# Large matrix products that read their moving operand in turn from the two halves of each row (attention and feed-forward, one core)

## The chip, the cores and the metric

The kernel runs on one core of a Trainium2 chip. The metric is device time in microseconds (us) of one execution. The unchanged kernel takes 863.88 us, the median of three runs (862.88 to 864.18).

## The reference

```python
def _attn_ref(q, k, v):                      # batch 8, heads 8, 576 rows, 64 columns
    q_s = softmax of q over its 64 columns
    k_s = softmax of k over the 576 rows
    kv = np.einsum('bhsd,bhse->bhde', k_s, v)
    return np.einsum('bhsd,bhde->bhse', q_s, kv)

def _moe_ref(x, w_in, w_out):                # x 4608 x 512, w_in 512 x 2048, w_out 2048 x 512
    h = np.maximum(x @ w_in, 0.0)
    return (h * h @ w_out)
```

The heads of the attention's output are put side by side, which gives x with 8 x 576 = 4608 rows of 512. All numbers are float32.

## The kernel before, in words

Nearly all of the time goes to the two products of the feed-forward part. Each float32 operand is split into a high and a low part of the type float32r, and a product is made of three matmuls, high times high, high times low and low times high. Every such matmul has a stationary operand of 128 x 128 (`lhsT`, loaded by its own LDWEIGHTS) and a moving operand of 128 x 512 (`rhs`), and adds into one PSUM bank of 128 x 512.

The batch is worked off in two ways.

- Tiles t = 0 to 6 are the first 512 rows of batches 0 to 6. For each tile a loop runs over the 16 blocks f of 128 hidden columns. `first_part` makes h (128 hidden columns x 512 rows of x) with x as the moving operand, `first` applies the relu and squares, `split_g` splits the square into `gh` and `gl`, and `second` adds into four banks `acc[c]` (128 rows of x each) with a block of 128 columns of `gh` or `gl` as the stationary operand and `w_out` (tile `w`, 512 output columns) as the moving one. `store` copies `acc[c]` to SBUF (tile `o`, on VectorE or ScalarE) and sends it to memory. The attention of the next tiles is worked in between.
- The remaining 1024 rows (batch 7 and the last 64 rows of the others) go through a seven-product scheme on quarters of the matrices. In the pair stage `product` (six matmuls, source line 1264) makes quarter products in the banks `z.A` and `z.B`; `pair_p1` to `pair_p7` copy them out on ScalarE (tile `u`) or add them on VectorE (tile `c`). In the closing stage `product_step` (twelve matmuls for two calls, source line 1780) does the same for `w_out` in the banks `out`; `copies`, `added` and `turned` take the results out, `turned` by a VectorE transpose that is followed by the stores.

The order of the work of tile 0 is made by a planner in the file (`Planner`, with fixed costs and a list of seeds); the rest stands in the order of the code. Engines wait for each other by semaphores alone. Matmuls that go through the planner's helper show source line 100, so tile names tell them apart: `h<-xh,w`, `h<-xl,w` (first product), `acc<-w,gh`, `acc<-w,gl` (second), `h<-...` at L1264 (pairs) and `out<-...` at L1780 (closing stage).

Of the kernel before, what the change touches and what calls it, by code (L numbers as in the profile page):

```python
# [15 lines left out]
AF = mybir.ActivationFunctionType  # L16
ALU = mybir.AluOpType
# [319 lines left out]
def attention_ffn(  # L337
# [26 lines left out]
    B, H, SQ, D = q.shape  # L364
    DM = H * D
    DF = w_in.shape[1]
    P = 128
    C = 4
    M = C * P
    TL = SQ - M  # L370
# [34 lines left out]
    TB = 2  # L405
# [3 lines left out]
    WT = B - 1  # L409
# [22 lines left out]
    V, S, G = Engine(plan, nc.vector, 0.14, 0.00108), Engine(plan, nc.scalar, 0.18, 0.00087), Engine(plan, nc.gpsimd, 0.1, 0.0021)  # L432
    T, Y = Engine(plan, nc.tensor, 0.013, 1 / 2400), Engine(plan, nc.sync, 0.1, 0.0)

    const.pool.tile([P, 32], F32, tag="pad", name="pad")
    ident = const.pool.tile([P, P], F32, tag="ident", name="ident")
    make_identity(nc, ident)
    ones = const.pool.tile([P, P], F32, tag="ones", name="ones")  # L440
# [33 lines left out]
    halves = [("i", f) for f in range(LA)]  # L474
# [63 lines left out]
    made = {}  # L538
# [490 lines left out]
    def first_part(t, f, x, p):  # L1029
        if p == 0:  # L1030
            made["h", f] = (
                View(Buffer(None, [P, M], F32, None, f"h_{t}_{f}", choices=[(ps_o, f"o{C - 1}")]))
                if t == 0 and f == LA else ps_h.tile([P, M], F32, tag="h", name=f"h_{t}_{f}")
            )
        xh, xl = x[p]
        with plan.together(True):
            for i, (w, m) in enumerate(((wi_h, xh), (wi_h, xl), (wi_l, xh))):
                T.matmul(
                    out=made["h", f], lhsT=w[f][:, p * P:(p + 1) * P], rhs=m,
                    start=(p == 0 and i == 0), stop=(p == NP - 1 and i == 2),  # L1040
                )
        if t == 0 and p == 0:
            plan.mark(f)
# [26 lines left out]
    def second(f, parts, acc, c, begin=0, end=NF - 1):  # L1070
        gh, gl = parts
        cs = slice(c * P, (c + 1) * P)
        with plan.together(True):
            for n, (a, w) in enumerate(((gh, wo_h), (gh, wo_l), (gl, wo_h))):
                T.matmul(
                    out=acc[c], lhsT=a[:, cs], rhs=w[f],
                    start=(f == begin and n == 0), stop=(f == end and n == 2),
                )

# [180 lines left out]
    def product(out, w, x, begin, end=True):  # L1260
        (wh, wl), (xh, xl) = (w[:, 0, :], w[:, 1, :]), x
        for k in range(2):
            for i, (a, m) in enumerate(((wh, xh), (wh, xl), (wl, xh))):
                nc.tensor.matmul(  # L1264
                    out=out.real(), lhsT=a[:, k * P:(k + 1) * P].real(), rhs=m[k].real(),
                    start=(begin and k == 0 and i == 0), stop=(k == 1 and i == 2),
                    skip_group_check=True,
                )

    def store(t, acc, c):  # L1270
        if c % 2 == 0:
            made["o"] = cvt.tile([P, 2, DM], F32, tag="w", name=f"o_{t}_{c}")
        o = made["o"][:, c % 2, :]
        if t == B and c == C - 1:
            V.tensor_copy(out=o[:, 0:DM // 2], in_=acc[c][:, 0:DM // 2])
            S.copy(out=o[:, DM // 2:DM], in_=acc[c][:, DM // 2:DM])
        elif c % 2 or 0 < t < WT - 1 and c == 0:
            S.copy(out=o, in_=acc[c])
        else:
            V.tensor_copy(out=o, in_=acc[c])  # L1280
        if t < B:
            rows = out[t * SQ:t * SQ + M, :].rearrange(
                "(p c) e -> p c e" if t < TB else "(c p) e -> p c e", c=C
            )
            Y.dma_start(out=rows[:, c, :], in_=o)
        else:
            per = P // TL
            for j in range(per):
                r0 = (c * per + j) * SQ + M
                queue = S if c == C - 1 and j % 2 else Y  # L1290
                queue.dma_start(out=out[r0:r0 + TL, :], in_=o[j * TL:(j + 1) * TL, :])


    load_kq(0, 0, "k")
# [295 lines left out]
    for t in range(WT):  # L1590
        x_next, acc = begin_next(t), begin_acc(t)
        parts = {}
        for f in range(NF):
            todo = turns[t, f]
            h = first(t, f, x)
# [75 lines left out]
    def pair_p1(z):  # L1671
        product(z.A, z.w["a11"], x_of["b11"], True)
        z.u1 = temp("xh2", f"u1_{z.n}")
        S.copy(out=z.u1, in_=z.A)

    def pair_p2(z):
        product(z.B, z.w["a12"], x_of["b21"], True)
        c = ffn.tile([P, M], F32, tag="r", name=f"c11_{z.n}")
        V.tensor_tensor(out=c, in0=z.B, in1=z.u1, op=ALU.add)
        square(c, V)  # L1680
        keep("b12", z.n, c)

    def pair_p6(z):
        product(z.A, z.w["s2"], x_of["t2"], False)
        z.u2 = temp(("xl2", "xl3")[z.n % 2], f"u2_{z.n}")
        S.copy(out=z.u2, in_=z.A)

    def pair_p5(z):
        product(z.B, z.w["s1"], x_of["t1"], True)
# [1 line left out]
    def pair_p7(z):  # L1691
        product(z.A, z.w["s3"], x_of["t3"], False)
        u3 = temp("xh3", f"u3_{z.n}")
        S.copy(out=u3, in_=z.A)
        c = temp("ek", f"c22_{z.n}", att, 2)
        V.tensor_tensor(out=c, in0=z.B, in1=u3, op=ALU.add)
        own_sums(z.n + 1, w_of.get(z.n + 1), 5)
        S.activation(out=c, in_=c, func=AF.Relu)
        square(c, S)
        keep("b21", z.n, c)  # L1700

    def pair_p4(z):
        product(z.A, z.w["a22"], x_of["t4"], False)
        c = ffn.tile([P, M], F32, tag="gh", name=f"c21_{z.n}")
        S.activation(out=c, in_=z.A, func=AF.Relu)
        square(c, S)
        keep("b22", z.n, c)

    def pair_p3(z):
        product(z.B, z.w["s4"], x_of["b22"], False)  # L1710
        c = ffn.tile([P, M], F32, tag="gl", name=f"c12_{z.n}")
        V.tensor_tensor(out=c, in0=z.B, in1=z.u2, op=ALU.add)
        z.c12 = c
        if z.n == PAIRS - 1:
            square(c, V)
        if z.n >= PAIRS - 2:
            raw["b11", J - 1] = raw.get(("b11", J - 1), ()) + (c,)
# [53 lines left out]
    def product_step(s, m, hold=False):  # L1771

        name, j = steps[s]
        hi, lo = split_of[s]
        fresh = name in ("b11", "b21", "t1")
        last = name == phases[-1]
        for i in range(2):
            wh, wl = weight(name, 2 * j + i)
            for k, (a, b) in enumerate(((wh, hi), (wh, lo), (wl, hi))):
                nc.tensor.matmul(  # L1780
                    out=banks[name][m].real(), lhsT=a[:, m * P:(m + 1) * P].real(),
                    rhs=b[:, i, :].real(), start=fresh and j == i == k == 0,
                    stop=(j == (2 if last else J - 1) and i == 1 and k == 2), skip_group_check=True,
                )

# [20 lines left out]
            else:  # L1806
                difference("t4", j, "b21", "t2", (to,))

    def turned(u, t, at, tag, bufs, queues):

        o = temp(tag, f"o_{t}_{at}", bufs=bufs)
        V.transpose(out=o, in_=u)
        per = TL // Q
        queues = itertools.cycle(queues)
        for a in range(P // Q):
            src = o[a * Q:(a + 1) * Q, :].rearrange("t (g d) -> t g d", d=Q)
            col = slice(at * P + a * Q, at * P + (a + 1) * Q)
            if t < B:
                rows = out[t * SQ:t * SQ + M, col].rearrange("(g t) d -> t g d", t=Q)
                next(queues).dma_start(out=rows, in_=src)  # L1820
                continue
            rows = out.rearrange("(b r) e -> b r e", r=SQ)
            for i in range(per):
                next(queues).dma_start(
                    out=rows[:, M + i * Q:M + (i + 1) * Q, col].rearrange("b t d -> t b d"),
                    in_=src.rearrange("t (b i) d -> t b i d", i=per)[:, :, i, :],
                )

    def copies(tags, banks_of, name):

        out = []
        for m, bank_of in enumerate(banks_of):
            u = temp(tags[m], f"{name}_{m}")
            S.copy(out=u, in_=bank_of)
            out.append(u)
        return out

    def added(bank_of, u, name):

        c = temp("r", name, bufs=None)  # L1840
        V.tensor_tensor(out=c, in0=bank_of, in1=u, op=ALU.add)
        return c

    differences = {
# [88 lines left out]
    for s in range(1, 6 * J):  # L1933
        for m in range(2):
            product_step(s, m)
        if s == J - 1:
            u1 = copies(("xh2", "xl2"), out_A, "out_u1")
        elif s == 4 * J - 1:
            u2 = copies(("xh3", "xl3"), out_A, "out_u2")
        elif s == 5 * J - 1:  # L1940
            u3 = copies(("xh1", "xl1"), out_A, "out_u3")
        if s < 5 * J + 3:
# [30 lines left out]
    for m in range(2):  # L1973
        for j in (0, 1, 3, 2):
            product_step(6 * J + j, m)
        turned(out_N[m], WT, m, "gh", None, (Y, S))


# [32 lines left out]
```

## Time and profile before

| | |
|---|---|
| median of three runs | 863.88 us |
| span of the profiled execution, first to last instruction | 861.0 us |
| what lies around the span (863.88 - 861.0) | 2.9 us |
| TensorE matmuls, busy | 849.3 us, 99% of the span |
| TensorE weight loads, busy | 697.4 us, 81% |
| VectorE, ScalarE, GpSimd, busy | 631.1, 425.0, 126.4 us |
| mean DMA traffic | 130 GB/s |

A matmul's busy time runs from its first read to the modelled end of its last write, and consecutive matmuls overlap, so the busy share does not tell how close TensorE is to its best. What tells it is the distance from the start of one matmul to the start of the next. Its clock was granted in full over nearly the whole span (2.4 GHz, the higher of its two levels).

### The profile page before, as it was taken

How to read it: one execution, taken by the hardware profiler on the slowest of the kernel's cores; microseconds unless marked ns; L12 is line 12 of the kernel's file. 1: busy time of each engine (PE TensorE's matmuls, PEld its weight loads, DVE VectorE, ACT ScalarE, POOL GpSimd, SP SyncE). 2: the span in 40 equal slices, each digit the busy share in tenths (PEclk: the TensorE clock that was granted, in tenths of full speed). 3: DMA queues.
4: the chain of work that ended last, by engine and by line, in shares of the span. 5: the costliest groups of instructions: out<-in, count | busy, mean ns of one | idle time of the engine just before them, and what ended most of it. 6: DMA issues, size and time to landing. Idle time of an engine off the chain costs nothing.

```text
span 861.0 us, 12692 instructions
## 1 busy us (share of the span) xinstructions
PE 849.3 (99%) x4356; PEld 697.4 (81%) x4356; DVE 631.1 (73%) x1241; ACT 425.0 (49%) x795; POOL 126.4 (15%) x154
## 2 busy tenths in 40 slices
PE   8899999999999999999999999999999999999997
PEld 7688888888888888888888888887888888888886
DVE  6999887776777667767777677676767746777885
ACT  5888864343534343433444353434434436676342
POOL 5899970000000000000000000000000000000000
PEclk9999999999999999999999999999999999999999
DMA  9991123322431444143332342133341049979465
GB/s 297 392 342 51 38 45 86 91 68 74 141 102 31 134 117 126 40 127 90 91 97 80 88 143 42 38 89 69 90 122 40 4 132 314 312 259 384 138 175 95
DMA packets 192752, 111.78 MB, mean 130 GB/s; under 512 B 130736, under 2 KB 175792, under 8 KB 192688
## 3 DMA queue, kind: packets, MB, share of 16 engines
q1 hardware_dynamic: 186768, 109.27, 43.1%
q10 hardware_dynamic: 5920, 1.71, 0.9%
q8 instruction: 34, 0.56, 0.3%
q14 instruction: 30, 0.25, 0.1%
HBM read 73.79 MB, written 36.57 MB: 128 GB/s over the span
## 4 chain that ended last, share of the span: by engine, by line
PE 91%; DVE 2%; DMA 1%; POOL 1%; SPq 1%; ACT 1%; issue 0%; DVEq 0%; ACTq 0%; POOLq 0%
PE acc L100 34%; PE h L100 34%; PE out L1780 9%; PE h L1264 9%; PE x L100 3%; PE kv L100 2%; SPq L100 1%; DVE bst L100 1%; DMA bst<-bst 0%; DVE q L100 0%; DMA k<-in_k_dram 0%; POOL w L100 0%; DVE km L100 0%; POOL qn L100 0%; PE qT L100 0%
## 5 line engine op out<-in xcount | busy, mean ns | idle before, releaser
L100 PE MATMUL h<-xh,w 128*128 128x512 f32 x896 | 296.9, 393 | 0.0
L100 PE MATMUL acc<-w,gh 128*128 128x512 f32 x888 | 276.1, 392 | 0.0
L100 PEld LDWEIGHTS h<-xh,w 128*128 128x128 f32 x896 | 168.2, 188 | 36.2
L100 PEld LDWEIGHTS acc<-w,gh 128*128 128x128 f32 x888 | 165.1, 188 | 34.8
L100 PE MATMUL h<-xl,w 128*128 128x512 f32 x448 | 175.1, 391 | 0.0
L100 PE MATMUL acc<-w,gl 128*128 128x512 f32 x444 | 173.7, 391 | 0.0
L100 DVE TENSOR_TENSOR gl<-h,gh 128x512 fp32r<-128x512 f32 x111 | 76.3, 688 | 59.5 <-ACT gh L100 51.3
L100 ACT ACTIVATE gh<-r 128x512 fp32r<-128x512 f32 x111 | 70.0, 631 | 78.6 <-PE acc L100 77.4
L100 PEld LDWEIGHTS acc<-w,gl 128*128 128x128 f32 x444 | 83.3, 188 | 18.4
L100 PEld LDWEIGHTS h<-xl,w 128*128 128x128 f32 x448 | 84.1, 188 | 17.2 <-DVE xl L100 0.2
L100 DVE SCALAR_TENSOR_TENSOR h<-h,r 128x512 f32<-128x512 f32 x112 | 77.2, 690 | 27.5 <-ACT r L100 26.6
L100 ACT ACTIVATE r<-h 128x512 f32<-128x512 f32 x112 | 66.5, 593 | 61.4 <-PE h L100 61.2
L100 POOL PARTITION_ALL_REDUCE kmx<-km x24 | 16.9, 705 | 510.7 <-DVE km L100 510.7
L1780 PE MATMUL out<-w,w 128*128 128x512 f32 x324 | 77.1, 393 | 0.0
L1780 PEld LDWEIGHTS out<-w,w 128*128 128x128 f32 x324 | 60.8, 188 | 13.9
L100 ACT ACTIVATE q<-q 128x576 f32<-128x576 f32 (+1 forms) x32 | 21.6, 674 | 69.8 <-DVE q L100 55.5
L100 DVE TENSOR_REDUCE bst<-q 128x18 f32<-128x576 f32 x48 | 35.9, 748 | 14.2 <-ACT q L100 13.5
L100 POOL TENSOR_TENSOR w<-w,raw 128x512 int32<-128x512 int32 x32 | 42.1, 1323 | 4.3 <-ACT raw L100 1.5
L100 POOL TENSOR_TENSOR w<-w,w 128x512 fp32r<-128x512 f32 x32 | 41.4, 1307 | 4.7 <-ACT w L100 4.1
L100 DVE TENSOR_TENSOR q<-q,bst 128x576 f32<-128x576 f32 x48 | 36.4, 758 | 1.7
L100 ACT ACTIVATE raw<-raw 128x1024 f32<-128x1024 f32 (+1 forms) x32 | 36.3, 1156 | 0.1
L1264 PE MATMUL h<-w,w 128*128 128x512 f32 x144 | 35.2, 392 | 0.0
(206 smaller groups left out, 1056.1 us busy)
## 6 DMA issues: line engine op xcount, KB each, us to landing
k<-in_k_dram SPq DMA_DIRECT2D x32, 256.0 KB, 2.9
raw<-in_moe_w_in_dram SPq DMA_DIRECT2D x16, 512.0 KB, 7.8
raw<-in_moe_w_out_dram SPq DMA_DIRECT2D x16, 512.0 KB, 9.0
w<-wo_sums SPq DMA_DIRECT2D x32, 256.0 KB, 3.9
w_sums<-w SPq DMA_DIRECT2D x30, 256.0 KB, 3.1
g_b<-c SPq DMA_DIRECT2D x30, 256.0 KB, 4.6
v<-in_v_dram SPq DMA_DIRECT2D x56, 128.0 KB, 3.1
out_dram<-o SPq DMA_DIRECT2D x28, 256.0 KB, 2.2
```

The lines of the kernel that those rows point to most:

```text
L100: getattr(self.eng, op)(*map(real, args), **{k: real(a) for k, a in kwargs.items()})
L1264: nc.tensor.matmul(out=out.real(), lhsT=a[:, k * P:(k + 1) * P].real(), rhs=m[k].real(), start=(begin and k == 0 and i == 0), stop=(k == 1 ...
L1780: nc.tensor.matmul(out=banks[name][m].real(), lhsT=a[:, m * P:(m + 1) * P].real(), rhs=b[:, i, :].real(), start=fresh and j == i == k == 0 ...
```

## The change

In every matmul with 512 moving columns the moving operand is read in another order: column 0, column 256, column 1, column 257 and so on, one from each half of the row in turn. The bytes and the number of columns stay the same. PSUM is still written in order, so a product's column 2b + a now holds column 256a + b. Three things put that right:

- copies and sums that take a result out of PSUM read it with a step of two elements, first the even places and then the odd ones (`in_rows`), and write SBUF in order;
- where the permuted columns are rows of x and become the stationary operand of the second product, block c of 128 holds 64 rows from each half of the tile, and `store` sends it to those rows;
- one result that is added to another in PSUM (`out_u2`) is left in the new order, and the last transposes read PSUM by `in_rows`.

On every engine the same instructions stand in the same order as before; only operand patterns differ. These are 3360 matmuls, 39 VectorE instructions (24 + 4 sums, 9 copies, 2 transposes), 57 ScalarE instructions (19 + 24 + 4 + 2 copies, 8 activations) and 20 of the 28 stores of `o`, whose target is 64 x 2 rows of 512 elements instead of 128 rows.

```diff
+    def in_turn(ap):
+        return ap.rearrange("p (a b) -> p b a", a=2)
+    def in_rows(ap):
+        return ap.rearrange("p (b a) -> p a b", a=2)
+    def as_rows(ap):
+        return ap.rearrange("p (a b) -> p a b", a=2)
...
-                    out=made["h", f], lhsT=w[f][:, p * P:(p + 1) * P], rhs=m,
+                    out=made["h", f], lhsT=w[f][:, p * P:(p + 1) * P], rhs=in_turn(m),
...
-                    out=acc[c], lhsT=a[:, cs], rhs=w[f],
+                    out=acc[c], lhsT=a[:, cs], rhs=in_turn(w[f]),
...
-                    out=out.real(), lhsT=a[:, k * P:(k + 1) * P].real(), rhs=m[k].real(),
+                    out=out.real(), lhsT=a[:, k * P:(k + 1) * P].real(),
+                    rhs=in_turn(m[k]).real(),
...
-        elif c % 2 or 0 < t < WT - 1 and c == 0:
-            S.copy(out=o, in_=acc[c])
+        if c % 2 or 0 < t < WT - 1 and c == 0:
+            S.copy(out=as_rows(o), in_=in_rows(acc[c]))
         else:
-            V.tensor_copy(out=o, in_=acc[c])
+            V.tensor_copy(out=as_rows(o), in_=in_rows(acc[c]))
...
+        rows = out[t * SQ:t * SQ + M, :]
+        if t < TB:
+            rows = rows.rearrange("(h p k) e -> h k p e", h=2, k=2)[c % 2, c // 2]
+            Y.dma_start(out=rows, in_=o)
         else:
+            rows = rows.rearrange("(a c b) e -> c b a e", a=2, c=C)[c]
+            Y.dma_start(out=rows, in_=o)
...
-        S.copy(out=z.u1, in_=z.A)
+        S.copy(out=as_rows(z.u1), in_=in_rows(z.A))
...
-        V.tensor_tensor(out=c, in0=z.B, in1=z.u1, op=ALU.add)
+        V.tensor_tensor(out=as_rows(c), in0=in_rows(z.B), in1=as_rows(z.u1), op=ALU.add)
...
-                    rhs=b[:, i, :].real(), start=fresh and j == i == k == 0,
+                    rhs=in_turn(b[:, i, :]).real(), start=fresh and j == i == k == 0,
...
-        V.transpose(out=o, in_=u)
+        V.transpose(out=as_rows(o) if halves else o, in_=in_rows(u) if halves else u)
...
-        turned(out_N[m], WT, m, "gh", None, (Y, S))
+        turned(out_N[m], WT, m, "gh", None, (Y, S), True)
```

The other copies and sums of the pair and closing stages change in the same way.

## Rows read from the trace of the kernel before

**Rows 1.** The page's busy times of the engines (busy us, share of the span, instructions) and the chain of work that ended last, by engine.

```profile
PE 849.3 (99%) x4356; PEld 697.4 (81%) x4356; DVE 631.1 (73%) x1241; ACT 425.0 (49%) x795; POOL 126.4 (15%) x154
...
PE 91%; DVE 2%; DMA 1%; POOL 1%; SPq 1%; ACT 1%; issue 0%; DVEq 0%; ACTq 0%; POOLq 0%
```

**Rows 2.** TensorE's waits (what waited, for whom: us in total, times, longest), all of them.

```profile
PE kT L100 <- DMA k<-in_k_dram: 1.7, 2, 1.0
PE idle L1458 <- POOL ident masks.py:199: 1.6, 1, 1.6
PE x L100 <- ACT kvh L100: 1.0, 2, 0.7
PE ekt L100 <- ACT kt L100: 0.8, 2, 0.6
PE qT L100 <- POOL qn L100: 0.8, 2, 0.6
PE ek L100 <- ACT k L100: 0.8, 1, 0.8
PE x L100 <- DVE kvl L100: 0.3, 1, 0.3
```

**Rows 3.** Pieces of the chain in order of time (start, us until the next piece starts, what, number of instructions). In this view consecutive matmuls count from start to start.

```profile
55.88 2.72 PE acc L100 x12
...
118.74 2.80 PE acc L100 x12
...
598.77 8.40 PE acc L100 x36
607.16 8.20 PE h L100 x36
...
706.12 70.05 PE h L1264 x306
...
781.63 74.82 PE out L1780 x324
```

**Rows 4.** Busy time and number of the instructions that write or read the tiles h, acc and out, in this order, over the whole span (stretch, its us, PE busy (count), PEld, DVE, ACT, granted clock, DMA share, GB/s).

```profile
0.00:861.00 861.00, 404.37 (x1680) 312.97 (x1680) 169.81 (x248) 85.23 (x144) 1.00 0.44 130
```

```profile
0.00:861.00 861.00, 328.10 (x1344) 250.73 (x1344) 6.20 (x9) 10.65 (x19) 1.00 0.44 130
```

```profile
0.00:861.00 861.00, 77.87 (x336) 63.07 (x336) 5.29 (x8) 4.60 (x8) 1.00 0.44 130
```

**Rows 5.** TensorE's instructions in order of time (start, us, what), around 21 and 25 us: 18 matmuls with 128 moving float32 columns, then five with 288 float32r columns, and a single one with 128.

```profile
21.08 2.13 PE L1458 MATMUL idle<-ident 128*128 128x128 f32 x18
...
25.27 0.30 PE L100 MATMUL x<-qh,kvl 128*128 128x288 f32 x1
25.40 0.29 PE L100 MATMUL x<-ql,kvh 128*128 128x288 f32 x1
25.53 0.30 PE L100 MATMUL x<-qh,kvh 128*128 128x288 f32 x1
25.66 0.30 PE L100 MATMUL x<-qh,kvl 128*128 128x288 f32 x1
25.80 0.29 PE L100 MATMUL x<-ql,kvh 128*128 128x288 f32 x1
...
26.90 0.27 PE L1458 MATMUL idle<-ident 128*128 128x128 f32 x1
```

**Rows 6.** A matmul and the weight load that runs beside it, in order of time, at 300 us.

```profile
300.16 0.40 PE L100 MATMUL h<-xl,w 128*128 128x512 f32 x1
300.16 0.19 PEld L100 LDWEIGHTS h<-xh,w 128*128 128x128 f32 x1
```

**Rows 7.** VectorE's groups by shape (count | busy us, mean ns | idle before): a reduction that reads each element from another place of the row (four places, 64 elements apart, in turn) and one that reads the row in order, both of 512 elements.

```profile
L100 DVE TENSOR_REDUCE km<-k 128x128 f32<-128x512 f32 x28 | 30.0, 1070 | 0.3 <-DMA k<-in_k_dram 0.3
...
L100 DVE TENSOR_REDUCE kc<-kT 128x1 f32<-128x512 f32 x4 | 2.7, 680 | 1.8 <-PE kT L100 1.8
```

**Rows 8.** VectorE's and ScalarE's groups that take products out of PSUM.

```profile
L100 DVE TENSOR_TENSOR c<-h,u 128x512 f32<-128x512 f32 x24 | 16.5, 689 | 16.3 <-ACT u L100 13.9 <-PE h L1264 2.2
```

```profile
L100 ACT COPY u<-h 128x512 f32<-128x512 f32 x24 | 14.0, 582 | 19.2 <-PE h L1264 19.2
```

**Rows 9.** The end of the chain.

```profile
849.96 6.49 PE out L1780 x28
856.45 0.02 issue
856.47 0.72 DVE o L100
```

**Rows 10.** Four stretches of the span: opening, tiles, pair stage, closing stage (stretch, its us, PE busy (count), PEld, DVE, ACT, POOL, granted clock, DMA share, GB/s).

```profile
0.00:39.00 39.00, 32.17 (x250) 27.27 (x251) 28.95 (x72) 27.22 (x60) 25.71 (x51) 1.00 1.03 339
39.00:700.00 661.00, 660.65 (x3429) 542.71 (x3428) 487.47 (x991) 312.87 (x594) 100.11 (x104) 1.00 0.33 91
700.00:781.60 81.60, 81.60 (x358) 66.90 (x357) 53.66 (x100) 52.33 (x101) 0.56 (x1) 1.00 0.87 291
781.60:856.40 74.80, 74.80 (x325) 60.50 (x323) 60.31 (x78) 32.61 (x43) 0.00 (x0) 1.00 0.66 188
```

More of the change, by code (lines that the diff above doesn't have):

```diff
@@ L1273, in store @@
         o = made["o"][:, c % 2, :]
-        if t == B and c == C - 1:
-            V.tensor_copy(out=o[:, 0:DM // 2], in_=acc[c][:, 0:DM // 2])
-            S.copy(out=o[:, DM // 2:DM], in_=acc[c][:, DM // 2:DM])
-        elif c % 2 or 0 < t < WT - 1 and c == 0:
-            S.copy(out=o, in_=acc[c])
-        else:
-            V.tensor_copy(out=o, in_=acc[c])
[L1281 to L1285, printed above, removed]
-        else:
[L1287 to L1291, printed above, removed]
+        if c % 2 or 0 < t < WT - 1 and c == 0:
+            S.copy(out=as_rows(o), in_=in_rows(acc[c]))
+        else:
+            V.tensor_copy(out=as_rows(o), in_=in_rows(acc[c]))
[3 more added lines that the diff above has]
+            Y.dma_start(out=rows, in_=o)
+        else:
+            rows = rows.rearrange("(a c b) e -> c b a e", a=2, c=C)[c]
+            Y.dma_start(out=rows, in_=o)
     load_kq(0, 0, "k")
@@ L1685, in pair_p6 @@
         z.u2 = temp(("xl2", "xl3")[z.n % 2], f"u2_{z.n}")
-        S.copy(out=z.u2, in_=z.A)
+        S.copy(out=as_rows(z.u2), in_=in_rows(z.A))
     def pair_p5(z):
@@ L1693, in pair_p7 @@
         u3 = temp("xh3", f"u3_{z.n}")
-        S.copy(out=u3, in_=z.A)
+        S.copy(out=as_rows(u3), in_=in_rows(z.A))
         c = temp("ek", f"c22_{z.n}", att, 2)
-        V.tensor_tensor(out=c, in0=z.B, in1=u3, op=ALU.add)
+        V.tensor_tensor(out=as_rows(c), in0=in_rows(z.B), in1=as_rows(u3), op=ALU.add)
         own_sums(z.n + 1, w_of.get(z.n + 1), 5)
@@ L1704, in pair_p4 @@
         c = ffn.tile([P, M], F32, tag="gh", name=f"c21_{z.n}")
-        S.activation(out=c, in_=z.A, func=AF.Relu)
+        S.activation(out=as_rows(c), in_=in_rows(z.A), func=AF.Relu)
         square(c, S)
@@ L1711, in pair_p3 @@
         c = ffn.tile([P, M], F32, tag="gl", name=f"c12_{z.n}")
-        V.tensor_tensor(out=c, in0=z.B, in1=z.u2, op=ALU.add)
+        V.tensor_tensor(out=as_rows(c), in0=in_rows(z.B), in1=as_rows(z.u2), op=ALU.add)
         z.c12 = c
@@ L1807, in make_t, with turned @@
                 difference("t4", j, "b21", "t2", (to,))
-    def turned(u, t, at, tag, bufs, queues):
+    def turned(u, t, at, tag, bufs, queues, halves=False):
         o = temp(tag, f"o_{t}_{at}", bufs=bufs)
-        V.transpose(out=o, in_=u)
+        V.transpose(out=as_rows(o) if halves else o, in_=in_rows(u) if halves else u)
         per = TL // Q
@@ L1827, in turned, with copies @@
                 )
-    def copies(tags, banks_of, name):
+    def copies(tags, banks_of, name, plain=False):
         out = []
@@ L1833, in copies @@
             u = temp(tags[m], f"{name}_{m}")
-            S.copy(out=u, in_=bank_of)
+            if plain:
+                S.copy(out=u, in_=bank_of)
+            else:
+                S.copy(out=as_rows(u), in_=in_rows(bank_of))
             out.append(u)
@@ L1840, in added @@
         c = temp("r", name, bufs=None)
-        V.tensor_tensor(out=c, in0=bank_of, in1=u, op=ALU.add)
+        V.tensor_tensor(out=as_rows(c), in0=in_rows(bank_of), in1=as_rows(u), op=ALU.add)
         return c
@@ L1938, in attention_ffn @@
         elif s == 4 * J - 1:
-            u2 = copies(("xh3", "xl3"), out_A, "out_u2")
+            u2 = copies(("xh3", "xl3"), out_A, "out_u2", True)
         elif s == 5 * J - 1:
```

## The prediction, made before the changed kernel was run

> **What bounds the kernel now.** I read the busy times and the chain first. TensorE is busy 99% of the span and carries 91% of the chain [rows 1]. The view of waits shows what it waits for: seven rows, 7.0 us together, all for tiles of the opening [rows 2]. After 39 us no other engine holds it up. So the time is the number of matmuls times the distance from one start to the next, and the next question is whether that distance is as short as it can be.
>
> The pieces of the chain give it. Twelve matmuls of 128 x 512 take 2.72 us at one place and 2.80 at another, 226.7 and 233.3 ns each; the same 36 take 8.40 us (233.3) for acc and 8.20 (227.8) for h; the two longest rows have 70.05 / 306 = 228.9 and 74.82 / 324 = 230.9 ns [rows 3]. At the granted clock, 2.4 GHz, 512 columns take 512 / 2.4 = 213.3 ns. So each matmul has 13 to 20 ns that are not columns. I take 229 ns as the mean, an excess of 15.7. There are 1680 + 1344 + 336 = 3360 of these matmuls [rows 4], so the excess is worth 3360 x 15.7 = 53 us. This is all that the change can win on TensorE, since the columns stay.
>
> **Where the excess comes from.** Three readings narrow it down.
>
> - It depends on the tiles: same shape, no wait, 226.7 against 233.3 ns [rows 3]. Something in reading the operands sets it, not the array.
> - It does not grow with the columns. Five matmuls of 288 columns start at 25.27 to 25.80, four distances of 132.5 ns; their columns take 120.0, so the excess is 12.5 [rows 5]. With 512 columns it is 13 to 20. What both have in common is a weight load of 128 columns that runs beside each matmul: it starts at 300.16 with the matmul and lasts 190 of its 230 ns [rows 6].
> - It is nearly absent where the moving operand is read slowly. Eighteen float32 matmuls of 128 columns take 2.13 us; less the length of a single one, 0.27, that is 109.4 ns for each of 17 distances, 0.855 ns per column, or 2.05 cycles [rows 5]. If two cycles per column are that form's own pace (106.7 ns), 2.7 ns are left, though weights are loaded beside it as well.
>
> My reading is that the moving stream and the weight stream get in each other's way in SBUF when the moving one walks through its row at full pace. Read in turn, each half of the row is walked at half pace, 0.83 ns per element, and that is the pace at which the trace shows the excess nearly gone. It is a reading, not a measurement: no row here has a float32r operand read in turn.
>
> **The change part by part.**
>
> *3360 matmuls read in turn.* Nothing in the trace shows this operation, so I bound it from both sides. The best is the columns alone, 213.3 ns: 3360 x 15.7 = 53 us won. The worst comes from two rows. A matmul that spends two cycles on a column takes 0.855 ns, 438 ns for 512 [rows 5], so 3360 x 209 = 702 us lost. A VectorE reduction that fetches every element from another place takes 1070 ns against 680 for one that reads in order, 0.76 ns more per element [rows 7]; added to each column that is 390 ns per matmul and 1310 us lost. Between these ends I take 216 ns: 213.3 and the 2.7 that the slowly read form keeps. That row is nearest, since it is TensorE's own, with weights loaded beside it, at the pace per half row that the change gives. About ten of the matmuls stand in the opening, where other engines hold TensorE [rows 2, 10], and win nothing. 3350 x 13 ns = 43.6 us won.
>
> The Trainium skill speaks against this: "SBUF — State Buffer", section "Door 1: The DMA port swizzle", says that SBUF has 16-byte lines, that at least two accesses must fall on a line for full bandwidth, and that each crossing to another line costs. Here every access would cross. The page gives no price; by the two-cycle row the sum would end near 1566 us instead of 823. No row here shows TensorE at it; the VectorE row of 1070 ns agrees with the page, for another engine and four places instead of two.
>
> *39 VectorE and 57 ScalarE instructions read PSUM with a step of two.* No row has that step. Below, they cost nothing, since the elements are as many; above, the 390 ns of the hopping reduction each [rows 7], which is 15 us on VectorE and 22 on ScalarE. VectorE is idle for 230 us of the span and ScalarE for 436 [rows 1], so this has to be looked at only where a bank is needed again soon. The tightest place is pair_p6: its copy of z.A takes 0.58 us [rows 8], at most 0.97, and pair_p7 writes that bank after one product of six matmuls, 6 x 216 = 1.30 us. It fits; if it did not, p7 and all behind it on TensorE would wait some tenths of a us in each of eight pairs. I cost it at nothing. Only the last transpose lies on the path: 0.72 us at the chain's end [rows 9], at most 1.1. I take the upper end, +0.4 us.
>
> *20 stores to 64 x 2 rows.* The bytes and the 2 KB rows are the same, and stores of o by tiles are followed by hundreds of us of matmuls: nothing. Nothing else moves on any queue.
>
> *What a faster TensorE meets.* Whoever feeds it gets 5.7% less time. Over the tiles DMA is at 0.33 and VectorE at 487 of 661 us; in the pair stage DMA is at 0.87, in the closing stage VectorE has 60.3 of 74.8 us, which becomes 85% of 70.6 [rows 10]. None is full on average, but the pair stage's loads can be late at single places. Between nothing and that whole stage's win, 81.6 x 0.057 = 4.6 us, I take 2.
>
> Sum: 861.0 + 2.9 around the span = 863.9, which is the runs' median; 863.9 - 43.6 + 0.4 + 2 = 822.7, **823 us**.
>
> **The rivals.**
>
> *Every column pays for its jump (slower).* Place: the moving read of all 3360 matmuls. Speaking for it: the VectorE pair of 1070 and 680 ns [rows 7]. Against: that read goes to four places in turn and belongs to another engine, and a fetch that is kept until its neighbours are used would serve both halves without a second access. At two cycles per column the time is 863.9 + 702 = 1566 us; a smaller price gives less. It decides early: the gain is gone when a column costs 15.7 / 512 = 0.03 ns more than at full pace. TensorE would then be the bound as before, with other engines idle longer.
>
> *The excess is fixed (no change).* It could belong to the change of weights in the array, about 13 ns for 288 and 512 columns alike [rows 3, 5], and the order of the moving columns would not touch it. Against it stands that it varies with the tiles by 7 ns. Time: 863.9 + 0.4 = 864.3 us. The same page of the Trainium skill, section "Who interferes with whom", says that TensorE has independent read ports for the moving operand and the weights and never waits on anyone. By that rule there would be no collision to remove, and the sum would be 864; the 7 ns by tile do not agree with it.
>
> *Only the part that varies by tile goes.* All matmuls come to 226.7 ns, the shortest of [rows 3]: 3350 x 2.3 = 7.7 us, less 0.4: 857 us. It is the weak end of faster.
>
> **How the numbers follow.** Changes below 0.2% (1.7 us) cannot be told from none here. I give the forecast mechanism 0.54 (810 to 845 us), its weak end 0.12 (845 to 862), no change 0.12, a small price per column 0.04 (866 to 868 and a little over), and the price of a jump in full 0.18. Faster is 0.66, same 0.12, slower 0.22. The range of 8 in 10 runs from the floor, 863.9 - 53 = 811 with 1 us to spare, through no change to a small loss, 868; what it leaves out is the full price of the jump.
>
> **What the changed profile would show.** Right: pieces of the chain with 12 large matmuls at 2.56 to 2.62 us, nearly the same for all tiles; the closing stage's 324 in about 70 us; the 288-column matmuls, which are untouched, still at 132 ns. VectorE's c<-h,u between 689 and 1080 ns. If large matmuls stand at 400 ns or more apart, the jump's price is right; at 227 to 233 as before, the excess is fixed. If they stand at 216 and the time is still above 835, new waits of TensorE in the last 160 us took it back.

## The result: 833.3 us, 30 us faster

The changed kernel takes 833.32 us (median of four runs, 832.5 to 833.55), the kernel before 863.38 us beside it (862.28 to 864.18). The ratio is 0.965, interval 0.964 to 0.967. The forecast was 823 us, so it was right on the direction and 10 us too low. The large matmuls became as short as forecast; a third of what they won came back as waits, most of it in a place that the prediction had not looked at.

The page of the changed kernel, its busy times and the chain by engine, which answer to [rows 1]:

```profile
span 831.5 us, 12703 instructions
PE 810.1 (97%) x4356; PEld 698.8 (84%) x4356; DVE 635.9 (76%) x1241; ACT 431.1 (52%) x795; POOL 125.4 (15%) x154
...
PE 73%; DVE 8%; DMA 4%; SPq 2%; ACT 2%; issue 1%; POOL 0%; DVEq 0%; ACTq 0%
```

Two things stand out. TensorE has lost 18 points of the chain, which other engines now hold in places. And VectorE and ScalarE are busy for 4.8 and 6.1 us longer, with the same number of instructions.

The pieces of the chain (start, us, what, number), as in [rows 3]:

```profile
148.98 2.59 PE h L100 x12
...
581.44 7.77 PE acc L100 x36
...
688.69 62.40 PE h L1276 x288
...
756.27 69.94 PE out L1786 x324
```

Each is 216 ns per matmul (2.59 / 12 = 215.8, 7.77 / 36 = 215.8, 69.94 / 324 = 215.9), whichever tiles are read. Before, the same places had 226.7 to 233.3.

TensorE's waits, of seventeen rows the ones that matter here (what waited, for whom: us in total, times, longest), as in [rows 2]:

```profile
PE x L100 <- ACT kvh L100: 2.6, 3, 0.9
PE x L100 <- DVE w L100: 1.7, 2, 1.1
PE idle L1464 <- POOL ident masks.py:199: 1.6, 1, 1.6
PE qTt L100 <- DMA k<-in_k_dram: 1.5, 1, 1.5
PE kmb L100 <- ACT dg L100: 1.1, 1, 1.1
...
PE h L1276 <- DMA ring<-w_sums: 0.5, 1, 0.5
...
PE kmb L100 <- DVE w L100: 0.4, 1, 0.4
PE h L100 <- POOL w L100: 0.4, 1, 0.4
```

All seventeen come to 15.4 us against 7.0 before; w is the converted weights, of which more below. Both kernels issue the same 4356 matmuls in the same order, so the two traces can be laid side by side, start by start. Distances that became a few ns shorter (the large matmuls) won 43.9 us. Distances that changed by much (waits, most of them new or longer, a few shorter) gave 13.6 us back on balance, 8.5 of them between 39 and 145 us, the time of tile 0; the opening before it comes out even. The rest came in small pieces, the largest at about 528, 585 and 669 us of the kernel before (0.2 to 1 us each, mostly the matmuls x waiting for kvh) and at 710 (0.6 us, for a transfer of ring). 863.4 - 43.9 + 13.6 = 833.1, which is the measured time to 0.2 us.

### The profile page after: what moved, and what is told of

It is laid out like the page before. It is cut to its first block, busy times and chain, and to the rows that moved or that the text cites. A ratio compares the mean times of both kernels' runs of the same rounds, so it can differ in the third digit from the quotient of the medians.

```text
span 831.5 us, 12703 instructions
## 1 busy us (share of the span) xinstructions
PE 810.1 (97%) x4356; PEld 698.8 (84%) x4356; DVE 635.9 (76%) x1241; ACT 431.1 (52%) x795; POOL 125.4 (15%) x154
## 4 chain that ended last, share of the span: by engine, by line
PE 73%; DVE 8%; DMA 4%; SPq 2%; ACT 2%; issue 1%; POOL 0%; DVEq 0%; ACTq 0%
PE acc L100 26%; PE h L100 25%; PE out L1786 9%; PE h L1276 8%; PE x L100 3%; SPq L100 2%; PE kv L100 2%; DVE bst L100 2%; DMA k<-in_k_dram 1%; DMA bst<-bst 1%; DVE km L100 1%; DVE up L100 1%; DVE w L100 1%; DVE q L100 1%; DVE gl L100 1%
## 5 line engine op out<-in xcount | busy, mean ns | idle before, releaser
L100 PE MATMUL h<-xh,w 128*128 128x512 f32 x896 | 286.8, 382 | 0.4 <-POOL w L100 0.4
L100 PE MATMUL acc<-w,gh 128*128 128x512 f32 x888 | 264.8, 380 | 0.1
L100 PE MATMUL h<-xl,w 128*128 128x512 f32 x448 | 170.0, 379 | 0.4 <-DVE xl L100 0.4
L100 PE MATMUL acc<-w,gl 128*128 128x512 f32 x444 | 168.4, 379 | 0.1
L1786 PE MATMUL out<-w,w 128*128 128x512 f32 x324 | 72.2, 379 | 0.0
L100 ACT ACTIVATE raw<-raw 128x1024 f32<-128x1024 f32 (+1 forms) x32 | 46.7, 1486 | 0.1
L100 DVE TENSOR_TENSOR bst<-bst 128x18 f32<-128x18 f32 (+1 forms) x96 | 17.9, 186 | 24.4 <-DMA bst<-bst 15.6
```

The costliest lines, as they stand in the source:

```text
L100: getattr(self.eng, op)(*map(real, args), **{k: real(a) for k, a in kwargs.items()})
L1786: nc.tensor.matmul(out=banks[name][m].real(), lhsT=a[:, m * P:(m + 1) * P].real(), rhs=in_turn(b[:, i, :]).real(), start=fresh and j == i ...
```

## What slowed tile 0

The chain of before from 40 to 130 us, by line:

```profile
by line: PE h L100 45.8%; PE acc L100 43.9%; PE x L100 3.5%; PE kv L100 3.3%; PE qT L100 1.9%; PE kmb L100 1.1%; PE kmT L100 0.5%; PE qTt L100 0.2%
```

And pieces of the chain of after in that time (start, us until the next piece, what):

```profile
83.75 0.64 DVE gl L100
84.39 0.78 DVE w L100
85.17 1.64 DVE up L100 x2
86.83 1.62 DVE w L100 x2
...
96.00 1.69 ACT raw L100
```

Before, the chain there is TensorE alone. After, it runs over VectorE's up and w and ScalarE's raw. These convert the weights: raw holds 64-bit words, and two ScalarE instructions (raw<-raw) and two VectorE ones (up<-raw, w<-raw,up) each read one half of every word, so they go through SBUF with a step of two 32-bit elements. GpSimd's w<-w,raw adds the other half, with the same step. The change did not touch any of them. The groups by shape over 37 to 130 us (count | busy us, mean ns | idle before), of before:

```profile
L100 ACT ACTIVATE raw<-raw 128x1024 int32<-128x1024 uint32 x14 | 16.1, 1152 | 0.1
L100 ACT ACTIVATE raw<-raw 128x1024 f32<-128x1024 f32 x13 | 15.0, 1152 | 0.0
...
L100 DVE TENSOR_SCALAR up<-raw 128x512 int32<-128x512 int32 x27 | 18.2, 685 | 0.1
...
L100 DVE TENSOR_TENSOR gl<-h,gh 128x512 fp32r<-128x512 f32 x14 | 9.6, 682 | 1.2 <-ACT gh L100 0.5
```

and of after:

```profile
L100 ACT ACTIVATE raw<-raw 128x1024 f32<-128x1024 f32 x13 | 21.0, 1616 | 0.0
L100 ACT ACTIVATE raw<-raw 128x1024 int32<-128x1024 uint32 x14 | 20.8, 1484 | 0.0
...
L100 DVE TENSOR_SCALAR up<-raw 128x512 int32<-128x512 int32 x27 | 22.1, 832 | 0.8 <-ACT raw L100 0.6
...
L100 DVE TENSOR_TENSOR gl<-h,gh 128x512 fp32r<-128x512 f32 x14 | 9.5, 682 | 0.9 <-ACT gh L100 0.2
```

The stepped instructions shown take 21 to 40% longer, with hardly any idle time ahead of them (w<-raw,up went from 682 to 805 ns); gl<-h,gh, which reads in order, takes 682 ns in both. GpSimd's w<-w,raw did not get longer in this time (1327 ns before, 1306 after), though it reads with the same step. Before 37 us, while the in-turn matmuls had hardly begun, raw<-raw takes 1162 to 1210 ns in the changed kernel too. So the suspicion is that a matmul that reads in turn slows the stepped instructions of VectorE and ScalarE beside it.

## The experiments

The four probes are the kernel before with blocks of extra matmuls behind its end; only the extra blocks are read. Distances are worked out as the start of a block to the start of the next, divided by its number of matmuls.

### The order of the columns, and the weights beside them

```diff
+    probe("pinorder", 0, row, w128)
+    probe("ptwo", 1, turn(2), w128)
+    probe("pfour", 0, turn(4), w128)
...
+    probe("ppairs", 0, turn(2, 2), w128)
+    probe("psteptwo", 0, lambda a: a.rearrange("p (b a) -> p a b", a=2), w128)
+    probe("pweightshalf", 1, row, lambda a: a[:, 0:P // 2])
+    probe("pweightsquarter", 0, row, lambda a: a[:, 0:P // 4])
+    probe("pshifted", 0, row, lambda a: a[:, 8:8 + P])
+    probe("ptwoshifted", 1, turn(2), lambda a: a[:, 8:8 + P])
```

> The kernel before, with fourteen blocks of 30 extra matmuls behind its last one, whose results nothing uses; each block reads its operands in another way. The mean distance from start to start in each block is looked at. Theory A (the moving stream collides in SBUF with the weight stream that runs beside it when it walks its row at full pace): in order 227 ns, in turn from two halves 216; with weights of 64 columns about 221 and of 32 columns about 218, since the excess goes with the length of the weight load; weights that lie 16 bytes apart, or shifted by 32 bytes, 230 or more in order; two halves with shifted weights still 216; 288 columns in order 132, in turn 122 to 123. Theory B (the moving stream has a limit of its own, whatever the weights do): 227 in order with any weights, 216 in turn, 288 columns 132 against 122. Theory C (a fixed cost of changing weights): 288 columns 132 in both orders. For four and eight places in turn: 216 if any number of places does, up to 438 (two cycles per column) if only two neighbours are kept. Pairs and runs of four from two halves: 216. Even places and then odd ones (a step of two, which walks the row at double pace): 227 or more.

TensorE in order of time (start, us, what):

```profile
862.75 6.64 PE L1987 MATMUL ptwo<-w,w 128*128 128x512 f32 x30
869.23 8.65 PE L1987 MATMUL pfour<-w,w 128*128 128x512 f32 x30
...
892.39 10.02 PE L1987 MATMUL ppairs<-w,w 128*128 128x512 f32 x30
...
909.75 13.70 PE L1987 MATMUL psteptwo<-w,w 128*128 128x512 f32 x30
923.26 7.07 PE L1987 MATMUL pweightshalf<-w,w 128*64 128x512 f32 x30
...
944.17 7.16 PE L1987 MATMUL pshifted<-w,w 128*128 128x512 f32 x30
951.17 6.64 PE L1987 MATMUL ptwoshifted<-w,w 128*128 128x512 f32 x30
```

In order a matmul stands 226.7 ns from the next. Two halves: 6.48 / 30 = 216. Four places 283, eight 489, pairs of columns 328, runs of four columns 250, a step of two 450. So other ways of scattering the read are dear, as the rival "every column pays for its jump" had it; the two halves alone are free. For pairs and runs of four 216 ns had been expected; they do not come near it.

On the weights the prediction's reading fails in part. If the excess came from the time in which both streams run, a load of 64 or 32 columns would shrink it. It does not: 231 and 232 ns. But where the weights lie does matter: 32 bytes further along, 233 ns in order and still 216 in turn; columns of weights 16 bytes apart, 235 in order. The excess goes with reading in order and not with the load's length. Every matmul of the probes has a weight load of its own, so whether the load is needed for the excess is not shown.

### The number of columns, and the distance of the halves

```diff
+        probe("pinorder" + name, 1, lambda a: a[:, 0:n], w128)
+        probe("ptwo" + name, 0, lambda a: a[:, 0:n].rearrange("p (a b) -> p b a", a=2), w128)
...
+        probe("papart" + name, (at + 1) % 2, apart(distance), w128)
...
+    probe("pquarterturn", 1, turn(2), lambda a: a[:, 0:P // 4])
```

> The kernel before, with blocks of 30 extra matmuls behind its last one, results unused. The first probe left two halves at 215.8 ns and in order at 226.7, but the excess in order did not shrink with the length of the weight load (230 with 64 columns of weights, 232 with 32), against theory A. 288 columns gained 9.4 ns by reading in turn, 512 columns 10.9. Looked at: in order and in turn with 448, 384, 256, 192 and 128 columns; two runs of 256 columns that lie 260, 264, 272, 288, 512 and 1024 elements apart; in turn with 32 weight columns; one and the same weights and moving row in order. Theory H (a cost at each matmul's start when the row is read in order, whatever its length): the difference between the orders is 9 to 11 ns for every number of columns. Theory I (a cost for each column or line): it goes with the columns, 10.9 ns at 512, 8.2 at 384, 5.5 at 256, 2.7 at 128. Theory A (collision with the weight stream, by its addresses): 32 weight columns in turn still 215.8, the same weights and row each time 226.7. Distance: 215.8 at every distance if two lines are kept wherever they lie; above that at 260, 264 or 272 elements if the place within 64 bytes matters.

TensorE in order of time, the blocks with 448 and with 128 columns, each in order and in turn:

```profile
864.46 6.24 PE L1987 MATMUL pinordera<-w,w 128*128 128x448 f32 x30
870.54 5.84 PE L1987 MATMUL ptwoa<-w,w 128*128 128x448 f32 x30
...
899.94 3.49 PE L1987 MATMUL pinordere<-w,w 128*128 128x128 f32 x30
903.27 3.51 PE L1987 MATMUL ptwoe<-w,w 128*128 128x128 f32 x30
```

From the starts of the matmuls, in order and in turn: 512 columns 226.7 and 215.8, 448 columns 202.7 and 189.1, 384 columns 174.4 and 162.4, 288 (in the first probe) 131.8 and 122.4, 256 columns 119.8 and 111.7. With 192 and 128 columns all stand at 111, so something other than the columns sets the distance there, and nothing is won. The difference from 256 columns up is 8 to 14 ns without a trend that would be proportional to the columns (theory I falls): it is a cost for each matmul, about as the prediction read it from 288 and 512 columns [rows 5]. At 256 columns in turn, 111.7 is already that floor of 111, so the 8 ns there may be cut short by it. How far the halves lie apart makes no difference (260 to 1024 elements, all within 2 ns of 216), and neither does a weight load of 32 columns beside reading in turn (216). The same weights and the same row each time stand at 228 in order, so a change of operands is not needed for the excess.

### Long runs from the two halves

What is it about the two halves: that each is walked at half pace, as the prediction has it, or only that the pattern is not one plain row? Long runs tell them apart.

```diff
+        ("pinorder", row), ("ptwo", turn(2)), ("prunsa", turn(2, 8)), ("prunsb", turn(2, 16)),
+        ("prunsc", turn(2, 32)), ("prunsd", turn(2, 64)), ("prunse", turn(2, 128)),
+        ("pgapa", gaps(2, 256, 264)), ("pgapb", gaps(4, 128, 136)), ("pgapc", gaps(16, 32, 40)),
```

> The kernel before with eleven blocks of 48 matmuls of 128 x 512 at its end, whose results are not used; beside each block ScalarE and VectorE run three or four stepped and as many unstepped instructions. Orders of the moving columns: in order; two halves in turn; runs of 8, 16, 32, 64 and 128 columns from the two halves in turn; and rows read in order but with gaps (two runs of 256 columns, four of 128, sixteen of 32, each followed by 8 words that are left out). Theory J, the reading of the prediction as far as it still stands: what saves the 11 ns is that each half is walked at half pace. A run of 8 or more columns is walked at full pace, so all of these stand at 226.7 ns or above (a little above where there are many runs: runs of four stood at 250, so about 238 for runs of 8 and 227 to 229 for runs of 64 and 128), and rows with gaps at 226.7 too. Theory K: the pace is not it; a matmul whose pattern is not one plain row (two dimensions in the access pattern) is set up in another way, so that long runs and rows with gaps stand at 216 like the two halves. Beside them, J expects ScalarE's stepped instruction to come down from 1650 ns (runs of four) towards 1140 as the runs grow; K says nothing on it. If a long run gives 216 ns and leaves the stepped instruction at 1140, there is an order that is fast and harmless.

```profile
864.58 11.04 PE L1987 MATMUL pinorder<-w,w 128*128 128x512 f32 x48
875.46 10.52 PE L1987 MATMUL ptwo<-w,w 128*128 128x512 f32 x48
885.82 11.84 PE L1987 MATMUL prunsa<-w,w 128*128 128x512 f32 x48
897.50 11.69 PE L1987 MATMUL prunsb<-w,w 128*128 128x512 f32 x48
...
931.30 11.04 PE L1987 MATMUL prunse<-w,w 128*128 128x512 f32 x48
942.18 11.20 PE L1987 MATMUL pgapa<-w,w 128*128 128x512 f32 x48
```

In order 10.88 / 48 = 226.7, two halves 215.8, and runs of 8, 16, 32, 64 and 128 columns 243, 240, 237, 228 and 227; rows with gaps 230 to 233. No long run wins anything, so it is not the form of the pattern (theory K falls). Of the orders from two halves, only the one that changes side at every column wins, which agrees with "half pace". It does not show that the pace is the cause: four places in turn change at every column too, walk each quarter still more slowly, and stand at 283 ns. The gaps cost 3 to 6 ns that theory J had not named.

### What reading in turn does to other engines

```diff
+        for i in range(3):
+            S.mul(out=step[:, :, i % 2], in_=step[:, :, i % 2].bitcast(F32), mul=0.5)
+        for i in range(3):
+            x = sa[:, 1024 * (i % 2):1024 * (i % 2) + 1024]
+            S.mul(out=x, in_=x.bitcast(F32), mul=0.5)
```

VectorE gets four stepped and four unstepped shifts in the same way, each beside a block of 48 matmuls.

> The kernel before, with blocks of 48 extra matmuls behind its last one; beside each block ScalarE and VectorE work on tiles of their own, first with a step of two elements in SBUF, then in order. Results are not used. In the changed kernel the weight conversion's ScalarE instructions with a step of two took 1442 and 1531 ns against 1156 before, VectorE's 786 and 810 against 683. Theory D (TensorE's reads in turn slow other engines' stepped reads of SBUF): beside matmuls in order ScalarE's stepped instruction takes 1150 to 1200 ns and VectorE's 685; beside two halves in turn 1450 to 1550 and 790 to 830; the unstepped instructions take the same beside all orders; with no matmuls beside, as beside matmuls in order. Rival E (those instructions were slowed by the loads or by GpSimd in the opening, whose times had moved): no difference between orders here. Pairs, runs of four and other orders: open; an order that keeps matmuls at 216 and the stepped instructions at 1160 would be the better one.

ScalarE's three stepped instructions as one group, first beside matmuls that read in order, then beside the two halves:

```profile
L100 ACT ACTIVATE w<-w 128x1024 fp32r<-128x1024 f32 x3 | 3.2, 1139 | 0.0
```

```profile
L100 ACT ACTIVATE w<-w 128x1024 fp32r<-128x1024 f32 x3 | 4.8, 1683 | 0.0
```

The stepped instruction goes from 1139 to 1683 ns, the unstepped one stays at 1050 (1046). VectorE's stepped shifts go from 692 to 918 ns, its unstepped ones stay at 695. That is the direction of theory D and somewhat more than the 1450 to 1550 and 790 to 830 ns that it expected; rival E falls. In tile 0 the changed kernel shows 1484 to 1616 and 832. Other orders, told by ScalarE's six instructions together (start, us, what), beside matmuls in order, two halves, pairs, and runs of four:

```profile
863.52 6.16 ACT L100 ACTIVATE w<-w 128x1024 fp32r<-128x1024 f32 x6
...
874.40 7.75 ACT L100 ACTIVATE w<-w 128x1024 fp32r<-128x1024 f32 x6
...
884.76 6.32 ACT L100 ACTIVATE w<-w 128x1024 fp32r<-128x1024 f32 x6
...
914.70 7.67 ACT L100 ACTIVATE w<-w 128x1024 fp32r<-128x1024 f32 x6
```

Beside four places and a step of two they take 6.17 and 6.14 us, with no matmuls beside them 6.13. So only the two halves and runs of four do much harm; VectorE's eight shifts say the same (6.69 and 6.48 us, 5.79 beside all the others). In the probe of long runs, which has the same six instructions, they take 7.65 us beside the two halves and 6.14 to 6.22 beside all the others. No order was both fast and harmless.

### Tile 0 read in order

The weights are converted during tile 0 and the opening only. So tile 0 alone goes back to reading in order, with its copies and stores as before; all later products read in turn.

```diff
-                    out=made["h", f], lhsT=w[f][:, p * P:(p + 1) * P], rhs=in_turn(m),
+                    out=made["h", f], lhsT=w[f][:, p * P:(p + 1) * P], rhs=m if t == 0 else in_turn(m),
...
-                    out=acc[c], lhsT=a[:, cs], rhs=in_turn(w[f]),
+                    out=acc[c], lhsT=a[:, cs], rhs=w[f] if acc is made["plain"] else in_turn(w[f]),
```

> The changed kernel, with tile 0 alone read in order as before (first and second product, copies and stores of tile 0 too); all else in turn. By the alignment of the two traces TensorE had lost 8.5 us to new waits by 145 us and won 5.4 us by shorter matmuls up to there. Theory F (the waits come with reading in turn in tile 0, where the weights are converted): waits fall back to those of before, ScalarE's conversions to 1157 ns, and the time is 833.3 + 5.4 - 8.5, about 830 us. Rival G (the waits come from the new copies, stores or from something else in the opening): the waits stay and the time is 833.3 + 5.4, about 839 us.

It takes 829.8 us (829.05 to 830.59), ratio 0.961, interval 0.960 to 0.963. The conversions are back to their old length (37 to 130 us; VectorE's up<-raw 684 ns), and the chain from 40 to 130 us is TensorE's again:

```profile
L100 ACT ACTIVATE raw<-raw 128x1024 int32<-128x1024 uint32 x14 | 16.0, 1146 | 0.0
```

```profile
by line: PE h L100 47.3%; PE acc L100 42.3%; PE x L100 3.5%; PE kv L100 3.3%; PE qT L100 1.9%; PE kmb L100 1.1%; PE kmT L100 0.5%; PE qTt L100 0.2%
```

Laid beside the kernel before, the large matmuls win 38.7 us, 5 less than in the changed kernel, and the waits give back 5.7 instead of 13.6; of these 1.4 stand in the first 40 us, and from there to 500 us no single one is longer than 0.15. So the slowed conversions cost more than tile 0's shorter matmuls were worth. The waits behind 145 us, 4.9 us in the changed kernel, stay (4.2 here).

To compare the two directly, both ran once more on one chip.

> The changed kernel once more, beside the next one on the same chip, to compare the two directly. Both theories that are left expect 833.3 us.

> The changed kernel with tile 0 read in order, beside the changed kernel on the same chip. If the gain of the first measurement is real it stands 3 to 4 us below the changed kernel, near 829.8 us; if it was scatter between two calls, the two stand within 1.7 us of each other.

The changed kernel took 832.81 us (832.33 to 836.6), this one 829.77 (829.15 to 831.48), 3.0 us less, and its slowest run is below the other's fastest. The forecast was 3 to 4. It beats both kernels.

### Tile 0 with shorter matmuls and nobody slowed

One doubt is left: tile 0 may have had no room for shorter matmuls in any case, since VectorE, ScalarE and GpSimd are busy there. So its matmuls were made shorter in another way, with 486 columns in order.

```diff
-                    rhs=m if t == 0 else in_turn(m),
+                    rhs=m[:, 0:486] if short else m if t == 0 else in_turn(m),
```

> The kernel with tile 0 in order (829.8 us, ratio 0.9614 to the kernel before), in which those matmuls of tile 0 that do not open a PSUM group have 486 columns instead of 512, so that they come about as close as matmuls in turn (216 ns) without reading in turn; 26 columns of tile 0 are left incomplete. About 364 matmuls lose 10.9 ns. Theory F (in the changed kernel the waits of tile 0 came from stepped instructions that reading in turn slowed): TensorE can use the shorter matmuls, 829.8 - 4.0, about 826 us, and ScalarE's conversions stay at 1157 ns. Rival L (at that pace TensorE overtakes whoever feeds it in tile 0, slowed or not): new waits take the gain, about 830 us.

It takes 828.28 us, but its runs reach from 827.29 to 831.85 us, and the ratio 0.961 (0.959 to 0.963) can't be told from that of tile 0 in order. By the time alone this is inconclusive. The trace says more. Against tile 0 in order, tile 0's matmuls win 3.4 us from 40 to 145 us, and about 0.8 us of it comes back there. The conversions stay as they were (37 to 130 us):

```profile
L100 ACT ACTIVATE raw<-raw 128x1024 int32<-128x1024 uint32 x14 | 16.1, 1147 | 0.0
```

So, in this one profiled execution, tile 0 could take most of what shorter matmuls win. With the two runs above, this puts the waits of tile 0 in the changed kernel down to the slowed conversions.

## Why the prediction was right, and where it was off

- **The term of the large matmuls: right.** 216 ns and 43.6 us were forecast, 215.8 ns and 43.9 us came. The pieces of 2.59 us, alike for all tiles, and the closing stage's 324 in 69.94 us are those it had asked to see. The 288-column matmuls, which were not changed, stand 130 ns apart at the place of [rows 5] (132.5 before).
- **The row that gave 216: in part luck.** It is 18 matmuls of 128 columns at 109.4 ns, read as a pace of two cycles per column with 2.7 ns left over [rows 5]. Each of them has a weight load of 128 columns of its own:

```profile
20.97 2.00 PEld L1458 LDWEIGHTS idle<-ident 128*128 128x128 f32 x18
```

  The probe's float32r matmuls of 192 and 128 columns, with such loads, stand at 111 ns, also when they are read in order. So the row does not show that its pace of reading set its distance, nor that 2.7 ns are what is left at that pace. The number came out; the way to it is not shown.
- **The reading behind it: half right.** That two halves in turn remove the excess came true, and the long runs agree with half pace; but four places, pairs and runs of four do not fit a rule by which slower walking is enough. That the weight stream is the other party stays open: the excess does not shrink with the length of the weight load and depends by some ns on its address. It is a cost of 8 to 14 ns for each matmul of 256 or more columns that reads in order; what makes it was not found.
- **"What a faster TensorE meets": mis-sized, and in the wrong place.** 2 us were set aside, with late loads in the pair stage in mind; 13.6 us came, 8.5 of them in tile 0. Two errors made this one. The stretch of tiles in [rows 10] averages tile 0 with six others. VectorE's 487 of 661 us looked loose there, but the same view for the time of tile 0 (stretch, its us, PE, PEld, DVE, ACT, POOL, clock, DMA, GB/s), of before and after, has it nearly full:

```profile
39.00:145.00 106.00, 106.00 (x553) 86.58 (x552) 91.49 (x167) 80.22 (x126) 82.97 (x80) 1.00 0.40 125
```

```profile
39.00:145.00 106.00, 100.37 (x538) 83.57 (x537) 97.40 (x166) 88.48 (x125) 82.16 (x80) 1.00 0.40 125
```

  And the durations of the other engines' instructions were taken as given. They were not: VectorE's 91.5 us became 97.4 and ScalarE's 80.2 became 88.5, with one instruction fewer each. The prediction named collisions of two streams in SBUF as its mechanism, but asked only what the change does to TensorE's own two. The other 5 us are of the kind that the term meant, a TensorE that comes too early for its feeders: 3.1 of them stand between 500 and 700 us, about half of that at two waits of x for kvh. Behind 145 us the mean of no group of the other engines' instructions grew by more than 15 ns.
- **The pair and closing stages: nothing came back worth naming.** One wait of 0.5 us for ring. They won what their matmuls won; the closing stage's VectorE, 60.1 of 69.8 us (86%), was no limit.
- **Reading PSUM with a step of two: free.** The sums c<-h,u took 688 ns (689 in [rows 8]), the copies u<-h 580 (582):

```profile
L100 DVE TENSOR_TENSOR c<-h,u 128x512 f32<-128x512 f32 x24 | 16.5, 688 | 12.3 <-ACT u L100 8.6 <-PE h L1276 3.6
```

  The last transpose stayed at 717 ns, so the +0.4 us set down for it was not needed. The 1070 ns reduction [rows 7] was a poor neighbour: it reads SBUF, from four places, and writes 128 results where the other writes one.
- **The stores: free**, as forecast. No wait of TensorE names one.
- **The rivals.** The jump's price of 702 us did not come for two halves, but is real for other orders: a step of two and pairs cost 224 and 101 ns per matmul, four places 56, runs of four 24. The Trainium skill, "SBUF — State Buffer", section "Door 1: The DMA port swizzle", asks for at least two accesses per 16-byte line. By that rule two halves would be slow; the runs do not agree for TensorE (216 ns against 227). Four and eight places go in the direction of the rule; pairs of columns and a step of two, with two accesses to each line, are slow against it. "The excess is fixed" and "only the part by tile goes" fall with 215.8 ns for all tiles.
- **The rule that no engine interferes.** The same page of the Trainium skill, section "Who interferes with whom", says that only the port pair that VectorE and GpSimd share causes contention. The traces do not agree: ScalarE's stepped instruction took 1139 ns beside one reading order of TensorE and 1683 beside another.

## What to carry to other kernels

Where TensorE is the bound, take the distance from start to start and compare it with the columns alone; where float32r matmuls with 256 or more moving columns stand 8 to 14 ns above what the order of two halves gives, that order is worth a try, with PSUM copies putting the order back, which cost nothing here. Then look stage by stage, not over the span, at who works beside TensorE: instructions of VectorE and ScalarE that go through SBUF with a step of two words may become slower, and in a stage where they feed TensorE the old order can be better. A change of access pattern on one engine has to be priced on its neighbours as well.

## What was not expected of the hardware

- Of all orders tried, two halves in turn alone made a 512-column float32r matmul shorter (227 to 216 ns); the others stood at 227 (runs of 128) to 489 ns (eight places).
- The same order slows SBUF instructions of ScalarE (1139 to 1683 ns) and VectorE (692 to 918 ns) that have a step of two words and leaves unstepped ones alone. Runs of four columns do so too; four places, pairs and a step of two do not. Why just these two is open. GpSimd's additions with that step (1327 and 1306 ns) and VectorE's reduction km<-k, which reads four places in turn (1062 ns before, 1047 after, behind 145 us), were not slowed.
- With 192 and with 128 columns the matmuls of the probe stood at 111 ns in either order.
